# A fused attention and gated-FFN kernel on one core: the first block's keys summed by TensorE, its values by GpSimd, and a new order of all units

## The chip, the cores and the metric

One core of one Trainium2 chip. The metric is device time in microseconds, the median of several executions; a profile is one further execution, recorded by the hardware. PE is TensorE (matmuls; PEld its weight loads), DVE is VectorE, ACT is ScalarE, POOL is GpSimd, SP is SyncE, which here only issues DMAs.

## The reference

```python
# q, k, v: (8 batches, 8 heads, 576 tokens, 64); pool = 8, so 72 keys a head
k_p = k.reshape(B, H, 72, 8, D).mean(axis=3)
v_p = v.reshape(B, H, 72, 8, D).mean(axis=3)
scores = matmul(q, k_p.T) / sqrt(D);  attn = softmax(scores)
x = matmul(attn, v_p)  ->  (4608 tokens, 512)
out = (sigmoid(x @ w_gate) * (x @ w_val)) @ w_out      # 512 -> 1536 -> 512
```

## The kernel before

The 4608 tokens are worked in nine blocks of 512. Blocks 1 to 8 go in pairs, by seven products of half-size matrices in place of eight. The first block, `first_pass`, goes alone and plainly, since nothing else can run yet. Each large product takes three matmuls (high by high, high by low, low by high), because every operand is split in a high part, rounded to the matmul's faster type (fp32r), and a low part, the remainder. The weights come as 64-bit numbers and are converted on chip in four steps a piece (`step`, names `raw`, `w`, `parts`).

The first block, heads in four pairs p = 0 to 3, runs thus:

- `first` loads the pair's keys, its queries, the values and a matrix of zeros and ones (`in_sums`).
- `keys` (L1232) sums eight tokens each: one VectorE reduction of 128x576 to 128x72 a pair. The layout has channels on partitions.
- `place_keys` (L1236) scales the sums into the block-diagonal tile `kbd`, two ScalarE instructions a pair.
- `scores` multiplies queries by `kbd` (tiles `sc`, two halves a pair); `maximum`, `exps` and `total` make the softmax on VectorE and ScalarE; `main` and `rest_parts` scale the probabilities, those of the first 64 keys (`main`) and of the last eight (`rest`) apart.
- `sum_v` (L1334) sums the values on TensorE with the matrix of zeros and ones, tokens on partitions: eight fp32 matmuls into `vp` for the first 64 keys of all pairs, four into `vr` for the last eight. `v_hi` and `v_lo` copy them out.
- `turn_main` and `turn_rest` transpose the probabilities on TensorE (`tp`, `tr`), `product_av` multiplies them by the values (`av`), `x_of` copies the result as x's high part into `xo` on ScalarE, and `x_low` (L1420) subtracts it from `av` on VectorE for the low part.
- Then the products with the weights begin: matmuls named `chain`. The first of them, `whole("G", 1, 0)`, needs both parts of x of pairs 0 and 1 in its first half and of pairs 2 and 3 in its second.

An fp32 matmul takes two passes of the array, so that the trace shows two records for each; an fp32r matmul takes one.

The order of the work is written out. The words of `ORDER` say in which order the first block's steps are recorded, and all instructions of the kernel are recorded as units in a list. `LATER`, a table of 3800 numbers, then says in which order these units are issued. Each engine runs its own instructions strictly in that order, waiting where an operand isn't there. All recorded instructions pass through one helper and so have one line, L317; they are told apart by their tiles. Tile names: `early` and `h` are regions that serve as the first block's workspace (queries, maxima, probabilities, sums), `raw` and `raws` are landing places, `pm` and `e` probabilities. At the start TensorE runs seven fp32 matmuls without use (`idle`).

Of the kernel before, what the change touches and what calls it, by code (L numbers as in the profile page):

```python
# [11 lines left out]
F32 = mybir.dt.float32  # L12
# [7 lines left out]
P = 128  # L20
# [30 lines left out]
SIZE = {"k": S, "q": BT, "V": DM, "R": DM, "U": 360}  # L51

PLACE = {"k0": (0, 0), "k1": (0, 576), "k2": (0, 1152), "k3": (0, 1728),
         "q0": (0, 2304), "q1": (0, 2816), "q2": (0, 3328), "q3": (1, 0), "V0": (1, 512), "V1": (1, 1024), "V2": (1, 1536),
# [7 lines left out]
TURNED = {4: ((0, 2), (2, 4)), 5: ((0, 2), (2, 3), (3, 4)), 6: ((0, 3), (3, 4)), 7: ((0, 3), (3, 4)), 8: ((0, 4),)}  # L62
SMALL = {1: 0, 6: 6, 7: 7}

ORDER = """
first.0.3 first.1.0 first.0.1 first.0.0 first.0.2 first.1.2 first.3.1 first.3.3 first.1.1 keys.0.3 first.3.0 first.2.0
put.0.3 first.3.2 first.3.4 keys.0.1 lw.0.0@0 keys.0.0 put.0.1 lq.2.3@0 first.1.3 keys.0.2 put.0.0 lw.1.1@1 lw.0.1@2
sc.0.0.1@0 put.0.2 lv.1.1@1 sc.0.0.0@1 max.0.0.1 lw.1.0@3 sc.0.2.0@2 max.0.0.0 exp.0.0.1 lk.1.1@9 sc.0.2.1@3 max.0.2.0
lq.2.2@2 sc.0.1.1@4 max.0.2.1 lq.1.0@3 sc.0.1.0@5 lr.2.0@4 max.0.1.1 max.0.1.0 exp.0.2.0 lr.1.0@5 exp.0.1.0 pv@6,7
exp.0.1.1 lq.1.2@6 exp.0.0.0 lk.2.2@10 lv.1.2@7 exp.0.2.1 sum.0.0 lk.1.0@11 lv.2.3@8 conv.0.0@5 conv.0.0 rest.0.0  # L70
sc.0.3.1@0 conv.0.0 main.0.0 vhi.0.3 sc.0.3.0@2 max.0.3.1 again.0.0 vlo.0.3 exp.0.3.1 rturn.0.0@5 max.0.3.0 main.0.1
turn.0.0@4 conv.0.0 rcopy.0.0 hi.0.0 exp.0.3.0 lo.0.0 kw.0.0 turn.0.1@1 lw.1.3@4 sum.0.1 hi.0.1 conv.1.1@6 conv.0.0@7
rest.0.1 vhi.0.0 conv.0.0 main.0.3 conv.0.0@8 vlo.0.0 again.0.1 vhi.0.2 rturn.0.1@3 lo.0.1 vhi.0.1 av.0.0@0 main.0.2
rcopy.0.1 vlo.0.1 turn.0.3@5 conv.1.0@9 conv.0.0 av.0.1@4 vlo.0.2 x.0.0 keys.1.1 turn.0.2@2 x.0.1 xl.0 hi.0.3 lr.1.1@9
xl.1 hi.0.2 conv.1.0 lo.0.3 lo.0.2 av.0.3@1 conv.0.1@10 conv.1.0 av.0.2@3 conv.1.0 x.0.3 x.0.2 xl.3 kw.1.0 conv.1.0@11
xl.2 ol.0@0 conv.0.1 conv.0.1 mm.0.1@6 conv.1.1 conv.0.1 conv.1.1 conv.0.1@12 kw.0.1 lw.0.2@3 conv.0.1 conv.0.1@13
# [34 lines left out]

LATER = """
6 5 4 7 0 11 3 2 21 8 25 27 19 28 14 18 23 31 22 20 9 26 13 35 17 36 33 1 10 40 45 76 39 37 12 48 47 52 16 55 32 66 38
41 53 67 30 62 42 58 29 68 63 61 43 15 64 83 54 74 46 88 75 71 80 72 98 137 85 124 78 113 110 112 81 89 101 100 97 102
99 60 84 92 105 106 90 82 107 73 131 108 79 115 128 116 120 111 94 126 93 117 96 95 59 121 87 198 104 129 139 206 141
122 145 144 103 143 205 123 142 136 86 138 130 158 91 109 148 119 146 204 125 135 133 154 155 156 153 134 152 132 223
140 162 150 167 149 165 127 163 157 217 164 151 147 168 159 190 171 160 170 244 175 161 166 56 172 191 169 178 180 173
174 118 179 57 194 187 181 231 182 224 183 245 234 200 197 207 203 201 193 202 210 186 185 34 189 226 50 192 196 177
184 176 237 188 241 248 235 240 227 239 251 246 252 218 260 249 258 283 243 254 213 259 280 253 284 277 65 262 233 287
268 238 212 270 44 279 51 257 275 220 269 255 278 219 267 266 232 276 273 242 281 222 300 289 299 285 229 306 228 230  # L120
286 293 114 303 290 282 294 256 236 274 291 295 317 304 247 301 327 333 305 330 302 334 336 288 312 319 332 331 328
329 318 335 199 308 353 309 307 310 315 261 313 323 316 326 363 325 354 209 365 292 324 367 346 314 340 347 339 349
366 322 350 297 400 341 311 361 351 216 69 377 362 406 343 298 359 342 215 344 70 345 264 368 296 383 356 348 338 374
265 371 381 225 271 375 272 376 337 378 372 387 357 386 355 388 358 396 399 373 397 394 412 398 49 404 393 403 392 208
369 413 401 364 418 407 411 408 420 370 405 379 410 402 419 389 417 390 409 414 415 425 321 427 320 448 426 24 424 382
428 380 263 447 430 423 385 421 435 384 195 422 445 431 221 458 438 436 432 579 467 484 437 442 486 444 453 450 452
493 211 429 470 471 468 469 494 465 214 462 463 464 451 433 434 498 487 391 441 501 488 416 449 502 439 457 585 485
472 499 473 481 482 491 440 459 518 478 474 503 250 483 479 461 480 514 466 522 492 475 500 476 455 454 531 591 489
532 533 528 511 490 477 523 525 395 446 529 526 686 524 505 508 530 527 541 496 547 497 506 517 546 460 515 520 507
495 456 512 443 535 545 543 534 504 578 513 542 552 549 521 536 557 519 558 550 559 77 583 597 568 561 569 571 537 572  # L130
612 570 565 544 604 575 581 551 573 582 607 352 566 556 516 567 555 562 613 540 563 574 577 605 608 633 564 606 598
580 601 553 599 584 539 609 538 602 603 649 600 623 624 560 554 643 630 628 670 360 637 576 679 629 673 954 660 657
676 589 592 680 614 586 634 587 668 677 661 590 596 594 595 667 681 588 593 674 610 615 611 678 509 671 616 622 675
625 619 631 627 510 698 635 617 690 701 618 636 632 638 620 621 691 626 640 650 644 685 672 683 695 702 654 653 641
687 646 688 647 651 652 699 656 700 703 658 704 692 693 663 639 648 642 696 655 697 682 712 709 659 669 664 645 715
694 662 727 705 716 666 548 730 707 728 665 708 710 711 713 684 718 719 721 723 720 714 726 725 706 722 731 732 729
738 736 744 724 953 761 734 762 746 748 955 737 747 739 753 740 749 741 756 763 745 769 733 766 764 956 752 759 760
776 757 758 765 768 767 783 806 751 754 772 994 755 807 1102 773 788 778 771 775 784 770 790 785 796 777 801 789 798
717 780 802 781 808 786 794 742 793 774 800 805 820 826 797 823 795 817 957 832 787 779 803 816 824 782 841 829 825
818 834 830 804 851 852 827 811 868 831 853 821 828 854 810 872 855 865 838 856 822 848 849 809 743 857 819 842 858  # L140
879 850 880 882 750 883 864 884 859 735 922 689 903 876 863 904 837 885 926 812 905 814 815 792 881 918 813 886 862
839 833 877 873 860 995 845 958 889 836 1057 844 997 846 890 843 866 921 887 867 869 892 959 900 891 993 871 906 861
1103 901 870 878 894 874 835 893 875 902 1104 840 962 1105 960 923 961 907 895 963 916 1107 896 996 924 979 1106 909
973 933 1049 980 925 1047 982 847 919 897 888 1048 898 974 910 942 899 934 908 912 939 943 983 935 1111 981 927 936
930 913 984 914 1112 937 1108 1113 950 791 1050 998 1109 920 1114 940 1110 999 1167 1000 1051 944 1003 1052 911 1001
1002 970 1058 928 1135 938 917 1023 1064 941 915 945 1024 1094 951 947 964 946 965 1059 948 952 966 1168 1028 985 967
1025 968 1027 1026 988 1169 1031 969 1172 1032 949 989 931 1010 1170 1014 932 1171 976 1471 986 1136 1060 1176 1011
1063 1075 1173 1041 971 1175 977 987 1174 799 990 1012 978 1018 1013 1042 1177 991 1179 1029 1134 972 992 1183 1137
1178 1033 1255 1043 1030 929 1061 975 1004 1076 1015 1069 1019 1053 1044 1138 1020 1005 1045 1080 1035 1021 1046 1016
1007 1070 1022 1054 1008 1006 1139 1055 1184 1065 1034 1038 1009 1140 1071 1062 1081 1085 1039 1072 1186 1090 1040  # L150
1125 1073 1086 1257 1082 1056 1074 1145 1095 1256 1182 1143 1258 1117 1247 1144 1017 1142 1083 1087 1036 1260 1115
1084 1118 1037 1066 1151 1261 1116 1067 1141 1262 1119 1088 1153 1152 1147 1128 1146 1154 1239 1068 1237 1155 1156
1238 1157 1077 1263 1158 1129 1078 1185 1098 1099 1187 1079 1096 1180 1188 1126 1190 1100 1120 1191 1159 1189 1259
1101 1192 1130 1121 1181 1097 1089 1201 1264 1240 1091 1164 1202 1211 1241 1265 1203 1204 1148 1131 1267 1161 1291
1127 1198 1206 1318 1132 1205 1212 1133 1221 1162 1219 1242 1220 1160 1163 1226 1222 1231 1199 1092 1214 1248 1193
1093 1334 1333 1243 1122 1266 1232 1165 1251 1123 1249 1253 1215 1217 1207 1166 1252 1149 1216 1150 1227 1278 1320
1218 1319 1472 1234 1223 1270 1228 1224 1194 1233 1229 1124 1299 1323 1321 1301 1335 1213 1235 1324 1371 1336 1268
1236 1250 1322 1300 1208 1338 1292 1269 1244 1337 1370 1339 1195 1281 1200 1196 1209 1272 1287 1197 1245 1305 1230
1282 1225 1283 1331 1246 1342 1343 1273 1340 1341 1275 1254 1332 1274 1352 1327 1276 1353 1295 1315 1362 1328 1306
# [167 lines left out]


@with_exitstack
def attention_then_ffn(ctx: ExitStack, tc: tile.TileContext, qT, kT, vm, vr, vn, sums8, wgv, wo, const, out, outT):  # L330
    book = Book()
    nc = Core(tc.nc, book)

# [258 lines left out]
    def load(*what):  # L592
        return fill(rawp.tile([P, S], F32, name="raw"), *what)
# [984 lines left out]
```

## Time and profile before

| | us |
|---|---|
| median of three runs | 905.88 (904.68 to 906.97) |
| the profiled execution, its own time | 906.25 |
| its span, first to last instruction | 904.5 |
| PE busy in the span | 893.6 (99%) |
| DVE busy | 657.4 (73%) |
| ACT busy | 497.1 (55%) |
| POOL busy | 199.4 (22%) |

The profiled execution's own time is 1.8 us above its span, and 0.4 us above the median of the runs. A busy time counts records whose ends are modelled, since matmuls are pipelined; a pace is better read from starts.

### The profile page before, as it was taken

To read this page: it belongs to the slowest core of one execution; us is meant where nothing else is said; L and a number is where in the kernel's file an instruction comes from. 1 tells how busy PE (TensorE), PEld (TensorE's weight loads), DVE (VectorE), ACT (ScalarE), POOL (GpSimd) and SP (SyncE) were. 2 spreads that over 40 slices of the span, in tenths; PEclk is the share of its full clock that TensorE was granted. 3 is DMA by queue.
4 is the path that set the end of the run, shared out by engine and by line. 5 is a ranking of instruction groups with operands and counts; after the bars stand their busy time and mean duration, and the time that the engine had idled before them with its cause. 6 is when DMAs were issued, how large, how long until landed. Compare 5 with 4: busy or idle time off the path is not lost.

```text
span 904.5 us, 12612 instructions
## 1 busy us (share of the span) xinstructions
PE 893.6 (99%) x4162; PEld 735.1 (81%) x4162; DVE 657.4 (73%) x1039; ACT 497.1 (55%) x1071; POOL 199.4 (22%) x369
## 2 busy tenths in 40 slices
PE   7999999999999999999999999999999999999998
PEld 6788778888888888888888888888888888888886
DVE  7989788889899998757678796356589552224863
ACT  5888887587856475445365554334355542224352
POOL 2412101011164235443343104132213000000000
PEclk9999999999999999999999999999999999999999
DMA  9899888889999888787987787686747775746644
GB/s 342 302 332 349 289 331 303 299 280 330 329 328 313 278 288 287 234 304 260 302 273 245 243 279 260 225 269 198 256 127 249 247 251 201 227 169 205 195 167 141
DMA packets 100289, 237.56 MB, mean 263 GB/s; under 512 B 13856, under 2 KB 34720, under 8 KB 98688
## 3 DMA queue, kind: packets, MB, share of 16 engines
q1 hardware_dynamic: 85040, 203.84, 66.7%
q0 software_dynamic: 15040, 32.79, 10.6%
q8 instruction: 33, 0.54, 0.2%
q14 instruction: 32, 0.26, 0.1%
q10 hardware_dynamic: 144, 0.13, 0.0%
HBM read 176.02 MB, written 60.69 MB: 262 GB/s over the span
## 4 chain that ended last, share of the span: by engine, by line
PE 90%; DVE 4%; DMA 3%; ACT 2%; issue 1%; SPq 0%; DVEq 0%; ACTq 0%
PE chain L317 55%; PE acc L317 27%; PE av L317 4%; PE sc L317 3%; DVE early L317 1%; DMA raw<-in_wgv 1%; DMA raw_o<-in_wo 1%; PE tp L317 1%; DMA raw<-in_vr 1%; DMA h<-in_kT 0%; ACT e L317 0%; DVE s L317 0%; DVE hs L317 0%; DVE h L317 0%; ACT hs L317 0%
## 5 line engine op out<-in xcount | busy, mean ns | idle before, releaser
L317 PE MATMUL chain<-xo,parts 128*128 128x512 f32 x2316 | 543.7, 392 | 0.0
L317 PEld LDWEIGHTS chain<-xo,parts 128*128 128x128 f32 x2316 | 430.7, 188 | 92.5 <-issue 1.0
L317 PE MATMUL acc<-hs,oparts 128*128 128x512 f32 x1008 | 237.3, 391 | 0.3 <-issue 0.2
L317 PEld LDWEIGHTS acc<-hs,oparts 128*128 128x128 f32 x1008 | 188.0, 188 | 40.9 <-issue 1.2
L317 POOL DMA_DIRECT2D turned<-turn x240 | 131.7, 551 | 214.8 <-DVE turn L317 185.2
L317 DVE TENSOR_TENSOR y<-chain,sV 128x512 f32<-128x512 f32 x46 | 31.1, 686 | 69.3 <-PE chain L317 59.0
L317 DVE TENSOR_TENSOR hs<-h,hs 128x1024 fp32r<-128x1024 f32 x52 | 63.0, 1217 | 11.6 <-ACT hs L317 11.4
L317 ACT CAST hs<-h 128x1024 fp32r<-128x1024 f32 x52 | 54.4, 1050 | 30.0 <-PE acc L317 23.1
L317 ACT COPY chain<-chain 128x512 f32<-128x512 f32 x46 | 26.4, 576 | 57.0 <-PE chain L317 47.3
L317 DVE TENSOR_TENSOR y<-chain,sG 128x512 f32<-128x512 f32 x46 | 31.2, 682 | 34.0 <-PE chain L317 23.4
L317 ACT CAST hs<-s 128x1024 fp32r<-128x1024 f32 x36 | 37.5, 1051 | 28.4 <-PE acc L317 13.0
L317 ACT COPY sG<-chain 128x512 f32<-128x512 f32 x46 | 26.7, 586 | 46.5 <-PE chain L317 44.8
L317 DVE TENSOR_TENSOR hs<-s,hs 128x1024 fp32r<-128x1024 f32 x36 | 43.8, 1219 | 11.2 <-ACT hs L317 10.9
L317 ACT COPY sV<-chain 128x512 f32<-128x512 f32 x46 | 26.7, 585 | 38.8 <-PE chain L317 36.1
L317 DVE SCALAR_TENSOR_TENSOR h<-gate,chain 128x512 f32<-128x512 f32 x46 | 30.6, 677 | 21.8 <-PE chain L317 21.7
L317 ACT ACTIVATE gate<-chain 128x512 f32<-128x512 f32 x46 | 26.9, 594 | 34.2 <-PE chain L317 31.7
L317 PE MATMUL sc<-kbd,raw 128*128 128x144 f32 (+1 forms) x262 | 41.2, 296 | 0.1
L317 PEld LDWEIGHTS sc<-kbd,raw 128*128 128x128 f32 (+1 forms) x262 | 33.6, 176 | 7.9 <-issue 2.8
L317 ACT ACTIVATE gate<-y 128x512 f32<-128x512 f32 x46 | 28.9, 633 | 19.1 <-DVE y L317 19.0
L317 PE MATMUL acc<-oparts,hs 128*128 128x512 f32 x144 | 38.7, 402 | 0.2 <-ACT oparts L317 0.2
L317 DVE TENSOR_REDUCE m<-sc 128x4 f32<-128x288 f32 x48 | 21.7, 452 | 18.2 <-PE sc L317 17.7
L317 DVE SCALAR_TENSOR_TENSOR h<-gate,y 128x512 f32<-128x512 f32 x46 | 31.0, 683 | 0.3
(211 smaller groups left out, 1073.8 us busy)
## 6 DMA issues: line engine op xcount, KB each, us to landing
oparts<-keptS SPq DMA_DIRECT2D x48, 512.0 KB, 4.4
oparts<-keptO SPq DMA_DIRECT2D x72, 256.0 KB, 4.2
raw<-in_wgv SPq DMA_DIRECT2D x12, 1024.0 KB, 8.5
out<-o SPq DMA_DIRECT2D x35, 256.0 KB, 3.6
raw<-in_kT SPq DMA_DIRECT2D x28, 288.0 KB, 5.0
raw<-in_qT SPq DMA_DIRECT2D x29, 256.0 KB, 4.7
raw<-in_vm SPq DMA_DIRECT2D x24, 256.0 KB, 5.6
raw_o<-in_wo SPq DMA_DIRECT2D x12, 512.0 KB, 8.1
```

What stands on the lines that cost most here:

```text
L317: return self._book.take(lambda: f(*args, **named))
```

## The change

Four things change, all in the first block but the last.

- The keys of batch 0 come with tokens on partitions (`in_kn`), and a new `keys` sums them on TensorE: five fp32 matmuls a pair, four over 128 tokens with 16 columns of ones and one over 64 tokens with eight. All four pairs write one PSUM tile, `kp`. ScalarE's `place_keys` reads that tile.
- The values of batch 0 come with channels on partitions, as those of the other batches do. GpSimd sums the first 64 keys' values in three halving additions (`v_tree`), the last split over the two heads: four instructions a pair, 16 in all, and four memsets (`clear_v`) before. The eight matmuls into `vp` and the four ScalarE copies go. The `vr` matmuls stay, with a smaller matrix.
- The low part of x: TensorE adds minus the high part to the PSUM bank of `av` (`x_less`, one fp32r matmul with a negated identity that `minus` makes on ScalarE), and ScalarE copies what is left. The four VectorE subtractions go.
- `ORDER` gets the new words, and `LATER` is another table of 3819 numbers. Rotating buffers (`raw`, `y`, `m`) get written-out places.

```diff
@@ -60,10 +61,11 @@
+LESSENED = (0, 1, 2, 3)
...
@@ -109,162 +111,169 @@
 LATER = """
-6 5 4 7 0 11 3 2 21 8 25 27 19 28 14 18 23 31 22 20 9 26 13 35 17 36 33 1 10 40 45 76 39 37 12 48 47 52 16 55 32 66 38
...
@@ -1230,8 +1251,24 @@
         def keys(j, p):
-            k = raws["k", j, p] if j else got[f"k{p}"].rearrange("p (g t) -> p g t", t=POOL)
-            nc.vector.reduce_sum(out=ks[j, p][:, :KEYS], in_=k, axis=AX.X)
+            if j:
+                nc.vector.reduce_sum(out=ks[j, p][:, :KEYS], in_=raws["k", j, p], axis=AX.X)
+                return
+            if "k" not in vp:
+                vp["k"] = ps.tile([P, PAIRS, KEYS], F32, name="kp", tag=CHAIN[5])
...
+            with book.unit():
+                for c in range(4):
+                    nc.tensor.matmul(
+                        vp["k"][:, p, 16 * c:16 * c + 16], lhsT=got[f"k{p}"][:, c * P:(c + 1) * P], rhs=ones,
+                        start=True, stop=True,
+                    )
...
@@ -1333,28 +1370,30 @@
         def sum_v():
 
-            vp["m"] = bank_for([P, PAIRS, 2, D], "vp")
...
+        def v_tree(p):
+            v = got[f"V{p}"].rearrange("p (d t) -> p d t", t=POOL)
+            for n in (4, 2):
+                nc.gpsimd.tensor_tensor(out=v[:, :, :n], in0=v[:, :, :n], in1=v[:, :, n:2 * n], op=ALU.add)
+            for r in (slice(0, D), slice(D, P)):
+                nc.gpsimd.tensor_tensor(
+                    out=vh0[p][r, r].rearrange("p (d t) -> p d t", t=1), in0=v[r, :, :1], in1=v[r, :, 1:2], op=ALU.add
+                )
...
@@ -1417,8 +1454,20 @@
+        def minus():
+            nc.scalar.activation(phs[0][:, :P], ident, AF.Copy, scale=-1.0)
+
+        def x_less(p):
+            t = xo[(1, 2)[p // 2]]
+            nc.tensor.matmul(
+                av[0, p], lhsT=phs[0][:, :P], rhs=t[:, 0, p % 2], start=False, stop=True, skip_group_check=True
+            )
+
         def x_low(p):
             t = xo[(1, 2)[p // 2]]
+            if p in LESSENED:
+                nc.scalar.copy(t[:, 1, p % 2], av[0, p])
+                return
             nc.vector.tensor_tensor(out=t[:, 1, p % 2], in0=av[0, p], in1=t[:, 0, p % 2].bitcast(F32), op=ALU.subtract)
```

TensorE's first instructions in the kernel before, from its start (`kbd_89` to `kbd_92` are the placed keys of pairs 0 to 3; `h` holds keys and queries):

```order
L317 MATMUL idle<-kbd_93 128x144 x7
L317 MATMUL sc<-kbd_89,h 128x144 x4
L317 MATMUL sc<-kbd_90,h 128x144 x4
L317 MATMUL sc<-kbd_91,h 128x144 x4
L317 MATMUL vr<-xs_220 96x2x64 x4
```

And TensorE's first instructions in the changed kernel; the pairs of the `kp` matmuls are 3, 0, 1 and, after the scores of two pairs, 2:

```order
L326 MATMUL idle<-kbd_93 128x144 x7
L326 MATMUL kp<-h 128x16 x4
L326 MATMUL kp<-h 128x8
L326 MATMUL kp<-h 128x16 x4
L326 MATMUL kp<-h 128x8
L326 MATMUL kp<-h 128x16 x4
L326 MATMUL kp<-h 128x8
L326 MATMUL sc<-kbd_89,h 128x144 x4
L326 MATMUL sc<-kbd_90,h 128x144 x4
L326 MATMUL kp<-h 128x16 x4
L326 MATMUL kp<-h 128x8
L326 MATMUL sc<-kbd_91,h 128x144 x4
```

Three units of key sums now stand ahead of the first scores. The third of them carries a wait for ScalarE's third event, which is `place_keys` of pair 0: it writes the PSUM tile that ScalarE reads there.

TensorE at the end of the first block in the kernel before, from the product of pair 1 to the first `chain` (`vres_107` belongs to pair 3, `vres_106` to pair 2; `sc` with `raw` are scores of the next block):

```order
L317 MATMUL av<-pr,vres_105 128x512
L317 MATMUL tr<-identr,r_262 96x128 x2
L317 MATMUL tp<-cst,early 128x128 x3
...
L317 MATMUL sc<-kbd_93,raw 128x144
L317 MATMUL av<-early_219,early 128x512
L317 MATMUL av<-other,vres_107 128x512
L317 MATMUL sc<-kbd_93,raw 128x144 x2
L317 MATMUL av<-early_219,early 128x512
L317 MATMUL av<-other,vres_106 128x512
L317 MATMUL chain<-xo_269,parts 128x512 x6
```

The same place in the changed kernel; `av<-xo_269,ph` are the new subtractions for pairs 0 and 1:

```order
L326 MATMUL av<-xo_269,ph 128x512
L326 MATMUL tr<-identr,r_262 96x128 x4
L326 MATMUL tp<-cst,early 128x128 x4
L326 MATMUL sc<-kbd_93,raw 128x144 x2
L326 MATMUL sc<-kbd_89,raw 64x144
L326 MATMUL sc<-kbd_93,raw 64x144
L326 MATMUL sc<-kbd_93,raw 128x144
L326 MATMUL av<-early_219,early 128x512
L326 MATMUL av<-other,vres_107 128x512
L326 MATMUL av<-early_219,early 128x512
L326 MATMUL av<-other,vres_106 128x512
L326 MATMUL chain<-xo_269,parts 128x512 x6
```

What stands between the last transposes and the first `chain` is the same work in another order; the two subtractions of pairs 0 and 1 stand ahead of these transposes, and the two of pairs 2 and 3 behind the first six `chain` matmuls.

GpSimd in the changed kernel, the last of its value sums (in the kernel before none of the `early` and `xs` rows is there; `kbd_93` is a key tile of the next block, whose sums VectorE makes):

```order
L326 TENSOR_TENSOR early<-early 128x64x4
L326 TENSOR_TENSOR early<-xs_220 64x64
L326 TENSOR_TENSOR early<-early 128x64x2
L326 TENSOR_SCALAR w_250<-w_250 128x1024
L326 TENSOR_TENSOR early<-early 64x64
L326 TENSOR_SCALAR kbd_93<-early 64x72 x2
L326 TENSOR_TENSOR early<-early 64x64
L326 TENSOR_SCALAR w_267<-w_267 128x1024
```

The last addition, which completes the values of pair 2, now stands behind a weight conversion and behind the placing of the next block's keys.

## Rows read from the trace of the kernel before

**Rows 1.** The page, part 1: busy us, share of the span, instructions.

```profile
PE 893.6 (99%) x4162; PEld 735.1 (81%) x4162; DVE 657.4 (73%) x1039; ACT 497.1 (55%) x1071; POOL 199.4 (22%) x369
```

**Rows 2.** Stretches A:B: length, busy us of each engine, clock, DMA share, GB/s.

```profile
7.20:27.30 20.10, 17.09 (x97) 12.51 (x96) 19.72 (x47) 14.04 (x30) 4.93 (x6) 1.00 1.03 382
27.30:904.50 877.20, 870.97 (x4047) 717.32 (x4045) 635.47 (x990) 480.55 (x1035) 191.81 (x343) 1.00 0.77 260
```

**Rows 3.** Timeline of PE: start, us, instruction, xcount [idle before <-releaser].

```profile
1.67 3.73 PE L317 MATMUL idle<-kbd 128*128 128x144 f32 x14 [1.67 <-POOL kbd L318]
5.30 3.28 PE L317 MATMUL sc<-kbd,h 128*128 128x144 f32 x16
9.74 1.25 PE L317 MATMUL sc<-kbd,h 128*128 128x144 f32 x8 [1.16 <-ACT kbd L317]
...
23.20 0.51 PE L317 MATMUL tp<-cst,early 128*128 128x128 f32 x3
...
24.61 1.02 PE L317 MATMUL av<-early,early 128*128 128x512 f32 x2
...
25.70 0.65 PE L317 MATMUL sc<-kbd,raw 128*128 128x144 f32 x4
26.20 1.02 PE L317 MATMUL av<-early,early 128*128 128x512 f32 x2
...
27.29 1.09 PE L317 MATMUL chain<-xo,parts 128*128 128x512 f32 x4
```

**Rows 4.** The chain that ended last, its first long piece: start, us, what.

```profile
2.12 4.28 DMA h<-in_kT
```

**Rows 5.** Timeline of DVE, first 28 us.

```profile
3.75 1.48 DVE L317 TENSOR_REDUCE early<-h 128x72 f32<-128x576 f32 x2 [3.75 <-DMA h<-in_kT]
6.42 0.75 DVE L317 TENSOR_REDUCE early<-h 128x72 f32<-128x576 f32 x1 [1.19 <-DMA h<-in_kT]
7.09 0.45 DVE L317 TENSOR_REDUCE early<-sc 128x4 f32<-128x288 f32 x1
...
8.32 0.74 DVE L317 TENSOR_REDUCE early<-h 128x72 f32<-128x576 f32 x1
...
20.99 0.68 DVE L317 TENSOR_TENSOR early<-early 128x512 f32<-128x512 f32 x1
21.70 0.29 DVE L317 TENSOR_TENSOR vres<-vr,vres 32x128 fp32r<-32x128 f32 x1
22.02 0.37 DVE L317 TENSOR_TENSOR r<-rest,r 128x128 fp32r<-128x128 f32 x1
...
23.88 0.43 DVE L317 CAST parts<-w 128x512 fp32r<-128x512 f32 x1
24.34 0.69 DVE L317 TENSOR_TENSOR xo<-av,xo 128x512 fp32r<-128x512 f32 x1
...
25.38 0.64 DVE L317 CAST parts<-w 128x512 fp32r<-128x512 f32 x1
```

**Rows 6.** Timeline of ACT, the first placing of keys.

```profile
4.61 0.53 ACT L317 ACTIVATE kbd<-early 64x72 f32<-64x72 f32 x2 [2.36 <-DVE early L317]
```

**Rows 7.** Timeline of PE at 84.8 us, the shortest fp32 passes of the trace.

```profile
84.83 0.33 PE L317 MATMUL av<-early 128*128 128x64 f32 x2
84.97 0.28 PE L317 MATMUL av<-other,vres 96*128 96x64 f32 x1
```

**Rows 8.** Timeline of POOL, 24 to 36 us.

```profile
24.46 1.27 POOL L317 TENSOR_TENSOR parts<-w,parts 128x512 fp32r<-128x512 f32 x1 [2.06 <-DVE parts L317]
...
28.26 0.38 POOL L317 TENSOR_SCALAR kbd<-early 64x72 f32<-64x72 f32 x1
...
32.84 1.47 POOL L317 TENSOR_SCALAR kbd<-early 64x72 f32<-64x72 f32 x1
```

**Rows 9.** Waits of PE over the whole span: waited for, us, times, longest.

```profile
PE tp L317 <- ACT y L317: 0.7, 1, 0.7
...
PE av L317 <- DVE pl L317: 0.5, 1, 0.5
```

## What I expect of the change

> **What bounds the kernel now.** I read the page's first part, then the table of stretches, then the waits, and only then the start. The page puts PE at 99% of the span [rows 1], so a wait elsewhere counts only if PE waits with it. The table splits the span at the first `chain`. From 27.3 to 904.5 PE is busy 870.97 of 877.20 us, at a granted clock of 1.00 [rows 2]: 6.2 us are idle, and these hold the tail behind the last matmul and the waits. The two longest single waits there are 0.7 and 0.5 us [rows 9]. So whatever the new table of numbers does behind the first block, it can't win more than these few microseconds. The first 27.3 us are the soft part: between 7.2 and 27.3 PE is busy 17.09 of 20.10 us, DVE 19.72 [rows 2]. DVE is the bound there, and the reader should see in its timeline that from 6.42 us on it hardly stops [rows 5]. Since the same products follow in either kernel, the prediction is first of all the start of the first `chain`, 27.29 us [rows 3].
>
> What starts DVE is a transfer. The third key tile takes 4.28 us and lands at 6.40 [rows 4]; DVE waits 1.19 us for it, reduces it at 6.42, and takes its first maximum at 7.09 [rows 5], though the scores for that were begun at 5.30 [rows 3]. GpSimd is busy 4.93 of these 20.10 us [rows 2]: it has room.
>
> **The change part by part.** *Keys on TensorE.* DVE loses three reductions ahead of the first maximum, and a fourth behind it (8.32, 0.74 us [rows 5]). In their place PE has five fp32 matmuls a pair, ten passes. It starts them behind the 14 idle passes, which go from 1.67 to about 5.2, 0.26 each, while four fp32 records of the same shape at full clock take 0.5 from start to start (25.70 to 26.20), 0.125 a pass [rows 3]: the start runs at the lower of the two levels, 1.2 GHz, and the record from 7.2 on shows 2.4 [rows 2]. The first scores are those of pair 0, and its sums stand behind those of pair 3: 20 passes before ScalarE can place it. No row shows a pass of 16 columns with 128 columns of weights. The nearest is one of 64 columns at full clock: two take 0.14 (84.83 to 84.97), 0.07 each [rows 7]. Lower bound: 0.07 for all, 1.4 us, done at 6.6. Upper bound: each costs as much as one of 144 columns at the clock of its time, 0.25 until 7.2 and 0.125 after, done at 8.7. I take the nearest row at the clock of its time, 0.14 until 7.2 and 0.07 after: 14 passes and six, done at 7.6.
>
> The rule in the Trainium skill that speaks to this is in "TensorE: Matmul & The Clock Gate", section "LDWEIGHTS (loading the stationary operand)": a weight load's time goes by its columns and not by what is streamed past, P/1.2 ns. By it a short stream doesn't make a short pass: 128 columns make 107 ns, and 20 passes 2.1 us, an estimate from that page; my 2.4 lies beside it, and the sum would be 0.3 us lower.
>
> Then ScalarE places pair 0 (0.53 for two instructions [rows 6], with 0.1 for each hand-over: 8.3). The third unit of sums, of pair 1, writes the PSUM tile that ScalarE reads, and by the order it waits for that; it stands ahead of the first scores on PE. So ten passes at 0.07 come next, to 9.0, and then four passes of scores at 0.125 [rows 3]: the first maximum at about 9.5. Before it was 7.09. **Start of DVE's run: +2.4.**
>
> *DVE's run.* From its first maximum to the end of the last 128x512 product of `main` it takes 14.58 us before (7.09 to 20.99 + 0.68 [rows 5]). After, one reduction of 0.74 is gone from it, and two steps that stood behind (`vres` 0.29, `r` 0.37 [rows 5]) stand within: 14.5. It ends at 24.0, in place of 21.67, if it is never kept waiting. But before, PE came to the last transposes only at 23.20 [rows 3], 1.5 us after DVE had finished; in the changed kernel PE will wait here, and start at 24.1. **Last transposes: +0.9.** From there to the first `chain` stood 4.1 us of work (23.20 to 27.29 [rows 3]); the same matmuls but for a few scores stand between them now, 3.9: first `chain` at 28.0. **+0.7.**
>
> *Values on GpSimd.* Eight matmuls into `vp` (16 passes) leave PE in a stretch in which it has 3 us to spare [rows 2]: worth nothing. On GpSimd an addition of 512 columns takes 1.27 where its operands are split in two types, and a scaling of 64x72 takes 0.38, or 1.47 in a worse moment [rows 8]. The tree has, for each pair, 256 columns, 128 and two of 64 rows by 64: by the share of columns about 0.65, 0.4 and 2x0.38, 1.8 a pair, 7.3 for four. The values land around 12 us, as the old ones did, so 19.5 to 21.6 with the weight conversion that stands between. The last addition, of pair 2, waits longer: it is queued behind the placing of the next block's keys, whose reduction DVE makes just ahead of its last product, at about 23.3. That gives 25.3 with three small instructions, and the product of pair 2 comes at 28.0 - 1.1 = 26.9. **Hidden, with 1.6 us to spare**; without that cover it costs what it is late.
>
> What GpSimd may cost is DVE's pace: one cast to `parts` takes 0.43 on DVE at 23.88 and 0.64 at 25.38, the second while GpSimd has its 1.27 addition [rows 5, 8]. If all 7.3 us of the tree slowed DVE like this, a third, that were 2.4; the tree's small pieces stand apart and DVE's reads of PSUM make half of its run, so the bounds are 0 and 1.5; I take **+0.4**.
>
> *Low part of x.* DVE loses four subtractions of 0.69 [rows 5], all behind its critical run; PE gets four fp32r matmuls of 512 columns, 0.27 each (four `chain` matmuls of that form: 1.09 [rows 3]). Two stand ahead of the last transposes, where PE waits anyhow; two behind the first `chain` matmuls. **+0.5**, between 0 (if a wait covers them) and 1.1.
>
> *The new table.* Some of the 1.2 us of the two named waits [rows 9] may go and as much may come: the order has no durations, so nothing there says which. Bounds -1.2 and +1.0; **-0.3**.
>
> Sum: 0.7 + 0.4 + 0.5 - 0.3 = +1.3, on the profiled execution's 906.25: 907.55. That execution is 0.37 above the median of the runs, so I state **907.2**.
>
> **The rivals.** *A, faster.* The start isn't late: the sums cost the lower bound (1.0 us less), GpSimd leaves DVE alone (0.4 less), and the 1.2 us of waits go. The chain of DVE's run can give back at most 0.7, since ahead of 23.2 PE was the later one; so 907.2 - 0.7 - 0.4 - 0.9 = 905.2, and 903.5 if subtractions and further small waits lie hidden too. For it: DVE has 2.7 us less work. Against: that work lies behind its run, or in the wait for the third key tile.
>
> *B, slower, by the clock.* Before, PE had scores of 144 columns from 5.30, then full clock at 7.2 [rows 2, 3]. After, it has in that time passes of 16 columns with little streamed, and a wait of 0.7 for ScalarE. If full clock comes only behind the first scores, the ten passes of pair 1 and the first scores run at 0.14 and 0.25: 0.7 + 0.5 later, and the six passes of pair 0 0.4 later, 1.6 in all: 908.8, or 909.6 if DVE's run waits for the next scores by as much as half of that again. It decides if the level is still 1.2 GHz at 11 us. [...]
>
> *C, slower, by GpSimd.* The tree takes twice my estimate, 14.6 us, as the 1.47 beside the 0.38 [rows 8] suggests. Then the last values come at some 28.9 and the product of pair 2 is 2 us late: 909.2. It decides at 8.9 us for the tree and its waits.
>
> **How the numbers follow.** Within 0.3% is 903.2 to 908.6, about what a measurement can tell here. Chances: my sum 0.5, A 0.25, B 0.15, C 0.10. A lies below 903.2 for half of its weight, 0.13 faster; B and C lie above 908.6 for most of theirs, with little of the sum's upper edge 0.21 slower; 0.66 within. The range takes in A's end and B's: 903.0 to 910.2; the sum's own is 905.5 to 908.9, by its terms' bounds taken together by halves.
>
> **What the profile would show.** Right: the first maximum at 9.5 (9.0 to 10.6), PE waiting for DVE ahead of the last transposes, the first `chain` at 28.0, the tree's 16 additions in about 7.3 us of busy time, DVE's long products at 0.68 beside it. Wrong: a first `chain` at 27.0 or earlier; PE waiting for GpSimd at a product of values; granted clock at half in the stretch from 7.2 to 11; or a difference in the table of waits behind the first block of more than 1.2 us, which my sum holds for impossible.

## The result and the profile after

The changed kernel took 914.33 us (median of 4, 911.83 to 917.89) against 905.28 for the kernel before on the same chip: a ratio of 1.0093, interval 1.0075 to 1.0111. It is slower, and by 9 us where 1.3 were forecast. The profiled execution took 911.83, its span 909.8; the other executions' spans go up to 916.1.

The page's first part, whose counterpart is [rows 1]:

```profile
PE 897.7 (99%) x4190; PEld 740.0 (81%) x4190; DVE 655.5 (72%) x1031; ACT 499.3 (55%) x1072; POOL 208.4 (23%) x389
```

TensorE has 4.1 us more work by it, GpSimd 9.0. Most of the loss shows in the start. The timeline of TensorE (columns as in [rows 3]):

```profile
1.67 3.52 PE L326 MATMUL idle<-kbd 128*128 128x144 f32 x14 [1.67 <-POOL kbd L327]
5.59 2.69 PE L326 MATMUL kp<-h 128*128 128x16 f32 x20 [0.41 <-DMA h<-in_kn]
8.90 2.42 PE L326 MATMUL kp<-h 128*128 128x16 f32 x10 [0.61 <-ACT kbd L326]
11.24 4.09 PE L326 MATMUL sc<-kbd,h 128*128 128x144 f32 x16
15.17 1.28 PE L326 MATMUL kp<-h 128*128 128x16 f32 x10
...
29.11 0.66 PE L326 MATMUL tp<-cst,early 128*128 128x128 f32 x4
...
32.63 0.47 PE L326 MATMUL av<-other,vres 96*128 96x512 f32 x1 [0.34 <-DVE vres L326]
...
34.03 1.56 PE L326 MATMUL chain<-xo,parts 128*128 128x512 f32 x6
```

Ten passes of the key sums cost 1.28 us in one place and 2.42 in another, though they are the same instructions. The table of stretches (columns as in [rows 2]) says why:

```profile
7.00:8.00 1.00, 1.00 (x9) 0.97 (x9) 0.00 (x0) 0.00 (x0) 0.00 (x0) 1.00 1.07 414
8.00:9.00 1.00, 0.39 (x3) 0.29 (x3) 0.00 (x0) 0.45 (x2) 0.00 (x0) 0.63 1.06 387
9.00:10.00 1.00, 1.00 (x6) 1.00 (x6) 0.00 (x0) 0.00 (x0) 0.00 (x0) 0.50 1.06 242
...
14.00:15.00 1.00, 1.00 (x6) 1.00 (x5) 1.00 (x4) 0.21 (x1) 0.65 (x3) 0.50 1.01 383
15.00:16.00 1.00, 1.00 (x10) 1.00 (x9) 0.75 (x3) 0.47 (x1) 0.33 (x1) 0.96 1.05 395
```

The granted clock was 1.00 (2.4 GHz) while the first twenty passes ran, fell to 0.50 (1.2 GHz) behind them, and came back at about 15 us, behind the scores of two pairs. In the kernel before it was 1.00 from 7.2 on [rows 2], and eight passes of scores took 1.25 us there [rows 3]. VectorE's timeline:

```profile
12.61 0.46 DVE L326 TENSOR_REDUCE early<-sc 128x4 f32<-128x288 f32 x1 [12.61 <-PE sc L326]
13.56 0.46 DVE L326 TENSOR_REDUCE early<-sc 128x4 f32<-128x288 f32 x1 [0.50 <-PE sc L326]
...
18.71 0.57 DVE L326 TENSOR_SCALAR early<-early 128x16 f32<-128x16 f32 x1
...
28.37 0.69 DVE L326 TENSOR_TENSOR early<-early 128x512 f32<-128x512 f32 x1
...
30.75 1.41 DVE L326 CAST parts<-w 128x512 fp32r<-128x512 f32 x1
32.19 0.29 DVE L326 TENSOR_TENSOR vres<-vr,vres 32x128 fp32r<-32x128 f32 x1
```

The sum from these lines and [rows 3, 5] (`early<-sc` is the first maximum, the product at 28.37 the last long one of the run): the first maximum is 5.52 us later (12.61 for 7.09). VectorE's run from there to the end of the last long product takes 16.45 in place of 14.58, +1.87. From that end to the first `chain` it is 4.97 (29.06 to 34.03) in place of 5.62 (21.67 to 27.29), -0.65. Together +6.74, which is the first `chain` at 34.03 for 27.29. Behind it stand 875.8 us to the end of the span, before 877.2; in all fifteen profiles of this case that stretch takes 875.5 to 878.3, wherever the first `chain` stands, so their spans differ mostly by the start.

### The profile page after: what moved, and what is told of

Same layout as the page of the kernel before. It is cut to its first block, busy times and chain, and to the rows that moved or that the text cites. A ratio compares the mean times of both kernels' runs of the same rounds, so it can differ in the third digit from the quotient of the medians.

```text
span 909.8 us, 12667 instructions
## 1 busy us (share of the span) xinstructions
PE 897.7 (99%) x4190; PEld 740.0 (81%) x4190; DVE 655.5 (72%) x1031; ACT 499.3 (55%) x1072; POOL 208.4 (23%) x389
## 4 chain that ended last, share of the span: by engine, by line
PE 92%; ACT 2%; DVE 2%; DMA 2%; issue 1%; POOL 0%; SPq 0%; DVEq 0%; POOLq 0%; ACTq 0%
PE chain L326 54%; PE acc L326 29%; PE sc L326 4%; PE av L326 4%; DMA raw<-in_qT 1%; PE kp L326 1%; PE tp L326 1%; DMA keptG0D<-parts 1%; DMA h<-in_kn 0%; DVE early L326 0%; DVE h L326 0%; ACT early L326 0%; DVE parts L326 0%; ACT e L326 0%; ACT w L326 0%
```

## The experiments

Each was timed against the kernel before on the same chip; its median in these runs was 905.65 to 906.57.

**The changed kernel again** (no edit), timed, and once more for a profile.

> The changed kernel once more, unaltered. In its first profile the granted clock is 0.50 from about 8.3 to 15.0 us, and the first chain stands at 34.03 in place of 27.29. Theory 1 (the clock: the key sums' passes let TensorE fall back to its lower level ahead of the first scores): the same fall is in this profile too, perhaps at another time, and the first maximum stands at 11 to 14 us. Rival (the fall was an accident of that one execution): the clock stays at 1.00 from about 7 us on, the first maximum stands at 10.5 to 11, and the time is near that of before plus 4.

> The changed kernel once more, for a third profile: its unprofiled times were up to 4 us above those of the two profiles. If the clock's first rise and its fall move from execution to execution, this profile shows another stretch at 0.50 and a span that follows it.

916.12 us, ratio 1.0107 (1.0087 to 1.0126). In both profiles the clock falls as in the first: 0.54 and 0.56 in 8 to 9 us, 0.50 to 14; the first `chain` stands at 33.64 and 33.45, +6.4 and +6.2. Of that the first maximum (11.85 and 11.87) makes +4.8, not +5.5: the first profile's key sums began 0.65 later, with a wait of 0.41 for keys that the two others don't have. VectorE's run takes 16.81 and 16.60. The fall is no accident. But it did not move in the third profile as that expectation held possible: what the executions with spans to 916.1 do differently is not seen in these three.

**Keys back on VectorE**, all else changed.

```diff
-            if "k" not in vp:
-                vp["k"] = ps.tile([P, PAIRS, KEYS], F32, name="kp", tag=CHAIN[5])
...
+            k = raws["k", j, p] if j else got[f"k{p}"].rearrange("p (g t) -> p g t", t=POOL)
+            nc.vector.reduce_sum(out=ks[j, p][:, :KEYS], in_=k, axis=AX.X)
...
-                    nc.scalar.activation(t[r, c], vp["k"][r, p], AF.Copy, scale=SCALE)
+                    nc.scalar.activation(t[r, c], ks[j, p][r, :KEYS], AF.Copy, scale=SCALE)
```

> The changed kernel with the keys summed by VectorE as before, all else as changed. Theory 1 and every theory that puts the loss on the key sums: first maximum at about 7.1 us, first chain at 26.5 to 27.5, and with the 875.8 us that stand behind the first chain in the changed kernel a time 0.5 to 3 us below before. Rival (the loss lies in the values on GpSimd, the low part or the new order): 908 or more.

909.89, ratio 1.0041 (1.0028 to 1.0054): 6.2 us below the changed kernel beside it, but not at or below the kernel before. The key sums are the larger part, not all. In TensorE's timeline one wait stands out:

```profile
6.77 2.20 PE L326 MATMUL sc<-kbd,h 128*128 128x144 f32 x16 [1.38 <-DMA h<-in_qT]
11.58 1.29 PE L326 MATMUL sc<-kbd,h 128*128 128x144 f32 x8 [2.61 <-ACT kbd L326]
```

The new order has no early place for the fourth reduction on VectorE. The clock then fell behind this wait, 0.50 from 13 to 19 us. First `chain` at 29.59.

**Wide passes**: the same key matmuls stream 128 columns, 16 of ones and 112 of zeros.

```diff
-            ones = got["k3"][:, 640:656]
+            ones = got["k3"][:, 640:768]
...
-                        vp["k"][:, p, 16 * c:16 * c + 16], lhsT=got[f"k{p}"][:, c * P:(c + 1) * P], rhs=ones,
+                        vp["k"][:, b + 16 * c:b + 16 * c + 128], lhsT=got[f"k{p}"][:, c * P:(c + 1) * P], rhs=ones,
```

> The changed kernel with the same key passes, each of which streams 128 columns (16 of ones, 112 of zeros) in place of 16. Theory 1 (the narrow streams let the clock fall): granted clock 1.00 throughout, a pass still near 0.13 us, first maximum at about 10.8 in place of 12.6, first chain near 31, 2 to 4 us faster than the changed kernel. Rival 2 (the loss is the 30 passes' price by their weights, the clock adds little): the same time as the changed kernel, within 1 us. Rival 3 (the clock falls for the waits between the units): it falls here as well.

912.13, ratio 1.0079 (1.0058 to 1.0099); the changed kernel beside it 1.0107, so the intervals overlap a little and the time alone is weak. TensorE's timeline isn't:

```profile
5.19 3.20 PE L327 MATMUL kp<-h 128*128 128x128 f32 x20
9.00 1.57 PE L327 MATMUL kp<-h 128*128 128x128 f32 x10 [0.62 <-ACT kbd L327]
10.50 2.23 PE L327 MATMUL sc<-kbd,h 128*128 128x144 f32 x16
...
31.86 1.57 PE L327 MATMUL chain<-xo,parts 128*128 128x512 f32 x6
```

```profile
11.29 0.95 DVE L327 TENSOR_REDUCE early<-sc 128x4 f32<-128x288 f32 x2 [11.29 <-PE sc L327]
```

The wait of 0.62 for ScalarE is still there, and yet the scores run at 2.4 GHz: sixteen passes in 2.23 us in place of 4.09. The first maximum came at 11.29, the first `chain` 1.6 to 2.2 us earlier than in the three profiles of the changed kernel. So the wait by itself doesn't bring the clock down (rival 3), and the passes' place and price stay when the clock is held: the first maximum is still 4.2 us late, in passes that are a little dearer (0.15 to 0.16 for 0.13). VectorE's run takes 15.59 here.

**A bank of their own for pairs 1 and 2.**

```diff
-                vp["k"] = ps.tile([P, PAIRS, KEYS], F32, name="kp", tag=CHAIN[5])
+                vp[side] = ps.tile([P, PAIRS, KEYS], F32, name="kp", tag=CHAIN[5 if p in (3, 0) else 4])
```

> The changed kernel with the sums of pairs 1 and 2 in a PSUM bank of their own, so that the third unit doesn't wait 0.6 us for ScalarE's placing of pair 0. Rival 3 (the wait breaks TensorE's work and brings the clock down): clock 1.00 and 3 us or more faster than the changed kernel. Theory 1: the clock falls all the same; 0 to 0.7 us faster.

913.84, ratio 1.0084 (1.0068 to 1.0100), overlapping with the changed kernel's 1.0087 to 1.0126; the first `chain` at 32.23. Without any wait between the thirty passes the clock fell all the same: 0.88 in 8 to 9 us, 0.50 from 9 to 12. It fell once more later, 0.60 in 22 to 24 us.

```profile
5.19 4.18 PE L326 MATMUL kp<-h 128*128 128x16 f32 x30
9.29 3.62 PE L326 MATMUL sc<-kbd,h 128*128 128x144 f32 x16
```

**One part alone on the kernel before.** Four kernels, each with one of the four changes.

> The kernel before with the keys of the first block summed by TensorE, nothing else changed and the order of before kept. Theory 1 (the key sums are the main cost, by their passes and by the clock that falls behind them): first maximum at 10.5 to 13 us in place of 7.09, 4 to 9 us slower than before. Rival (the keys cost what was forecast, about +1, and the loss comes only with the new order): 0 to 2 us slower.

Keys (the code of the diff ahead of the prediction, the order of before): 918.51, ratio 1.0136 (1.0123 to 1.0149). This is more than the part can be charged with: the matrix of ones comes in pair 3's tile, which the old order loads last, and TensorE waits for it. The clock was 0.50 from 9 to 25 us.

```profile
8.13 2.38 PE L318 MATMUL kp<-h 128*128 128x16 f32 x10 [3.04 <-DMA h<-in_kn]
```

> The kernel before with the values of the first block summed by GpSimd, nothing else changed; the 16 additions stand in GpSimd's order where the changed kernel has them. Theory 2 (GpSimd's additions slow the VectorE instructions beside them and hold back GpSimd's placing of the next keys): first chain 0.5 to 2 us later than 27.29, time 0.5 to 2 us over before. Rival (the additions are hidden): within 0.5 us of before.

Values on GpSimd (`v_tree`, `clear_v`; the eight `vp` matmuls go): 909.61, ratio 1.0044 (1.0027 to 1.0060). The first `chain` came at 30.48, in a profiled execution that was the fastest of the seven (907.77). Here TensorE was idle where the value sums had stood, and its clock fell:

```profile
21.16 1.09 PE L318 MATMUL tp<-cst,early 128*128 128x128 f32 x4 [2.73 <-DVE early L318]
```

```profile
18.00:20.00 2.00, 0.43 (x4) 0.29 (x4) 1.87 (x5) 2.00 (x5) 1.76 (x4) 0.84 1.03 350
20.00:25.00 5.00, 3.85 (x8) 2.25 (x9) 4.93 (x8) 2.55 (x6) 4.70 (x8) 0.50 0.99 400
```

> The kernel before with the low part of x made by TensorE and ScalarE, nothing else changed; each subtraction and copy stands where the VectorE subtraction stood. Four more matmuls of 0.27 on a TensorE that is nearly always busy: 0 to 1.2 us over before. Rival (VectorE's four freed 0.69 us let the next scores start earlier): up to 1 us under before.

Low part (`minus`, `x_less`, copies on ScalarE): 908.42, ratio 1.0028 (1.0018 to 1.0039). First `chain` at 28.73, and TensorE then waits for ScalarE's copies (columns as in [rows 9]):

```profile
PE chain L319 <- ACT xo L319: 0.8, 2, 0.5
```

Not all of the 1.44 us at the first `chain` are the low part's: 0.37 are a key transfer that landed later (first maximum 7.46), 0.29 VectorE's run (14.87), and only 0.78 lie behind it, where its new matmuls begin. TensorE ran at the lower level to about 10 us in this start, 24 passes of scores in 5.34 us, though nothing of the low part stands there and the table of stretches says 1.00:

```profile
6.12 5.34 PE L319 MATMUL sc<-kbd,h 128*128 128x144 f32 x24 [0.72 <-DMA h<-in_qT]
```

> The new order of all units with the keys on VectorE, the values on TensorE and the low part on VectorE, as before. With the keys alone undone the new order was 3.8 us over before, its scores of the third pair waiting 2.6 us for a late key reduction and the clock falling behind that wait. Theory 3 (the new order, drawn up for other work, costs this, whatever does the values): 2 to 4 us over before, with the same wait. Rival (the values on GpSimd and the low part make these 3.8): within 1 us of before.

The new order with none of the three: 919.04, ratio 1.0150 (1.0131 to 1.0170). This tells nothing of the order that the changed kernel has: I had to find places for the four copies of the value sums, which the new order lacks, and put them on ScalarE ahead of the exponentials. There VectorE waits 5.04 us:

```profile
26.09 0.75 DVE L330 TENSOR_REDUCE early<-early 128x8 f32<-128x576 f32 x1 [5.04 <-ACT early L330]
```

I count this one as failed. Whether the new order costs or wins in itself was not settled.

**Sums later**: only those of pair 0 ahead of the first scores, with narrow and with wide passes. In `LATER` the sums of pair 1 move behind the scores of pair 0, those of pairs 3 and 2 behind the scores of pair 1; pair 3 gets a bank of its own.

```diff
...
+            bank = "k3" if p == 3 else "k"
+            if bank not in vp:
+                vp[bank] = ps.tile([P, PAIRS, KEYS], F32, name="kp", tag=CHAIN[4 if p == 3 else 5])
```

> The changed kernel with only the sums of pair 0 ahead of the first scores; those of pair 1 stand behind these, those of pairs 3 and 2 behind the scores of pair 1 (pair 3 in a bank of its own). 20 passes and the wait for ScalarE go from ahead of the first maximum. Theory 1 (the place and the price of these passes, in the start that DVE waits for): first maximum at 8 to 9.5 in place of 12.6 or 11.5, first chain 2.5 to 4 us earlier, 2 to 4 us faster than the changed kernel (910 to 913). Rival (the loss lies behind the start: GpSimd beside VectorE and a clock that falls later): less than 1 us of it comes back.

> The same with passes of 128 columns in place of 16. Theory 1 with the clock: 1.00 from its first rise on, first chain as in the run beside it or up to 2 us earlier. Rival (the clock does not matter once the scores stand between the sums): the same time, within 1 us.

Narrow: 918.09, ratio 1.0129 (1.0111 to 1.0147). Wide: 912.73, ratio 1.0070 (1.0054 to 1.0087). The intervals are apart: 5.4 us for the columns alone. TensorE, narrow:

```profile
5.19 2.25 PE L331 MATMUL kp<-h 128*128 128x16 f32 x10
8.05 2.29 PE L331 MATMUL sc<-kbd,h 128*128 128x144 f32 x8 [0.62 <-ACT kbd L331]
10.13 2.25 PE L331 MATMUL kp<-h 128*128 128x16 f32 x10
...
22.43 2.02 PE L331 MATMUL vr<-xs 64*96 64x128 f32 x8
```

and wide:

```profile
5.16 1.46 PE L332 MATMUL kp<-h 128*128 128x128 f32 x10
7.24 1.25 PE L332 MATMUL sc<-kbd,h 128*128 128x144 f32 x8 [0.62 <-ACT kbd L332]
8.33 1.46 PE L332 MATMUL kp<-h 128*128 128x128 f32 x10
```

Eight passes of scores take 2.29 us in the first and 1.25 in the second: 1.2 and 2.4 GHz. With narrow passes TensorE never left the lower level until about 27 us, and I had expected this kernel to be faster than the changed one. Theory 1 in the form "place and price" was wrong in what it forecast here (the first maximum at 9.42 came 2 to 3 us earlier, the time went up), and right in the form "clock". The wide one had its first maximum at 8.04, yet its first `chain` only at 32.62, for VectorE then waits for scores behind the sums that stand between, and after that 1.24 and 0.68 for ScalarE: an earlier first maximum alone gives little.

```profile
11.20 0.95 DVE L332 TENSOR_REDUCE early<-sc 128x4 f32<-128x288 f32 x2 [1.48 <-PE sc L332]
```

Nor did the clock hold here "from its first rise on": it was 0.55 in 22 to 24 us and 0.60 in 24 to 26. That fall cost little: from the end of VectorE's run (27.51) to the first `chain` it is 5.11 us, 4.98 in the run with wide passes, where the clock held.

**Values on GpSimd, with work in TensorE's gap**: eight matmuls of the same size, unused, where the value sums stood.

```diff
+                            vp["m"][:, :, hd], lhsT=ident,
+                            rhs=got[f"q{c}"].rearrange("p (n h d) -> p n h d", h=2, d=D)[:, :, hd],
```

> The values alone on GpSimd, as run before (4.0 us over the kernel before, granted clock 0.50 from 19.7 to 26 us), with eight matmuls put back on TensorE where the value sums stood: the same size, on queries and the identity, their result unused. Theory 4 (the value sums that went had kept TensorE busy; without them the clock falls): clock 1.00 in 18 to 27 us, 2 to 3.5 us faster than without them. Rival (GpSimd's additions beside VectorE are the cost): within 1 us of the run without them.

908.85, ratio 1.0037 (1.0020 to 1.0053), not to be told from 1.0044 without them. The clock was 1.00 from 7 us on, the first `chain` at 29.98 in place of 30.48. So the fall of the clock there was real, but worth at most half a microsecond at the first `chain`, of which 0.17 stood already at the transposes ahead of it (20.99 for 21.16); the rival holds. The 2.7 us that remain at the first `chain` have their lines on GpSimd and VectorE:

```profile
26.56 0.90 PE L318 MATMUL sc<-kbd,raw 128*64 128x144 f32 x4 [1.10 <-POOL kbd L318]
```

```profile
22.71 1.33 DVE L318 TENSOR_TENSOR r<-rest,r 128x128 fp32r<-128x128 f32 x1
```

The next block's keys are placed behind the additions, so that its scores wait; and the `r` subtraction, 0.37 before [rows 5], takes 1.33 beside GpSimd's work. That work is not an addition but a weight scaling (22.86, 1.03 us), which stood at 16.04 in the kernel before and now comes behind the additions.

**Keys on VectorE with the old start**: as the second experiment, but transfers, reductions and placings in the order of before.

> The changed kernel with the keys on VectorE as before, and this time the first transfers, the key reductions and the placings in the order of before (the fourth reduction behind two maxima). In the earlier run without this the third pair's scores waited 2.6 us and the clock fell behind the wait. Theory 5 (beyond the key sums, the values on GpSimd and the low part on TensorE cost of themselves, 2 to 4 us): 908 to 910, with the first scores of the third pair near 10 us and no wait of 2.6. Rival (the late fourth reduction was the rest of the loss): within 1 us of before, 905.5 to 907.5.

908.86, ratio 1.0023 (1.0013 to 1.0034): without the late reduction 2.3 of the 3.8 us remain, with the keys out of play. Not all of that is the values' and the low part's own: the first scores wait 1.45 us for queries here, and the clock is low behind that. First `chain` at 29.93.

```profile
6.64 1.22 PE L331 MATMUL sc<-kbd,h 128*128 128x144 f32 x8 [1.45 <-DMA h<-in_qT]
```

```profile
12.00:16.00 4.00, 4.00 (x17) 3.45 (x17) 4.00 (x12) 1.53 (x6) 2.59 (x5) 0.50 1.00 384
```

No kernel tried beats the one before.

## Why the prediction was wrong

**The step that failed first** is "the nearest row at the clock of its time", 0.14 until 7.2 and 0.07 after, and on it "the first maximum at about 9.5". I took a pass of 64 columns as the measure of one of 16. Measured at 2.4 GHz: 20 passes from 5.59 to 8.28 and ten in 1.28, 0.13 each; at 1.2 GHz ten in 2.42, 0.24. That is what a pass of 144 columns takes (0.125 [rows 3] and 0.26): the columns streamed were not the price. The weight loads (PEld) fill nearly all of the time, nine of them 0.97 us of the stretch from 7 to 8, which makes them the likely price; no run had other weights. The 0.07 of [rows 7] was read from a place where they don't show: there the two loads begin while the long matmuls ahead still run.

```profile
84.38 0.62 PE L317 MATMUL acc<-oparts,hs 128*128 128x512 f32 x2
84.61 0.41 PEld L317 LDWEIGHTS av<-early 128*128 128x128 f32 x2
```

For the first twenty the lower level that I assumed hid the error (2.4 for 2.69, and a start 0.4 late for a transfer); for the third unit it stood bare, "ten passes at 0.07". The Trainium skill's rule ("TensorE: Matmul & The Clock Gate", "LDWEIGHTS (loading the stationary operand)") goes by the columns of the weights, 107 ns for 128. The trace agrees in kind, with about a fifth more at 2.4 GHz (0.13), and not at 1.2 GHz, where a pass took 0.24. I had named it and weighed it for the twenty alone; for the ten of the third unit it makes 1.1 in place of my 0.7, an estimate from that page. The upper bound, "as much as one of 144 columns", held for the twenty, done at 8.3 for 8.7.

**The clock** is rival B, with a chance of 0.15. It decided as written, "if the level is still 1.2 GHz at 11 us": it was 0.50 there in all three profiles of the changed kernel. Its course was another. I let the rise come late; in the profiles it came in time, fell behind the first twenty passes and stayed down through the third unit (2.42 us, for 1.28 at 2.4 GHz) and the first scores (1.37 us from their start to the first maximum, for 0.79 in the run with wide passes). The differences are 1.1 and 0.6, together 1.7 us of the first term. B has 1.6 for it, which is near by luck: 0.4 of that stood for six passes of pair 0 that ran at 2.4 GHz. First maximum 12.61, +5.5 (+4.8 in the two other profiles), where my sum and B together made +4.0. The rest of the term is the passes and their wait: the wide passes, with the clock held, still leave +4.2. The Trainium skill says ("TensorE: Matmul & The Clock Gate", Part 1) that throttled is the clock's default and that activity releases it. The two "sums later" runs agree with that in part: in the wide one TensorE came to 2.4 GHz ahead of the first scores, in the narrow one it stayed at 1.2 GHz to about 27 us, though no wait there was longer than 0.62 us.

**VectorE's run** was put at 14.5 and took 16.45. It waits for scores at the lower clock (0.50 at 13.56), which the run with wide passes doesn't; that one took 15.59. Part of the rest is single operations that stretch beside GpSimd's additions (0.57 for the 128x16 scaling, 0.17 in the run with wide passes). My +0.4 stood for this; the 1.1 that is left with the clock held lies under its upper bound of 1.5. The term "last transposes +0.9" followed these: 29.11.

**From there to the first `chain`** I counted 3.9 and it took 4.92: the product of pair 3 waits for `vres`, which stands behind the cast of 1.41 us, 0.43 and 0.64 before [rows 5]. A weight scaling on GpSimd (30.85, 1.03 us) runs beside it. The order showed the place, not the length.

**Hidden value sums.** "Worth nothing" for the matmuls taken from TensorE missed that a gap on TensorE went with a lower clock; alone, that was half a microsecond at most. The additions themselves came out near the forecast 7.3 us, 7.9 by GpSimd's rows, and the last ended in time:

```profile
29.86 1.01 POOL L326 TENSOR_TENSOR early<-early 64x64 f32<-64x64 f32 x1
```

The product of pair 2 came at 32.93, so rival C fell. What costs is beside them: the values alone 4.0 us (2.4 to 5.4). The low part, forecast at +0.5, cost 2.8 alone (1.6 to 3.5), in an order not drawn up for it; its profile shows less (0.8 ahead of the first `chain`, two waits of 0.8 together behind).

**The new table**: behind the first `chain` 875.8, and 878.2 and 877.7 in the two other profiles of the same kernel, before 877.2. A gain of 0.3 can't be seen in that. Rival A fell with the start.

**What stays open**: the medians lie 2.5 us above the changed kernel's profiled times. Spans of 914 to 916 with a recorded mean clock of 1.00 look like the narrow "sums later" run, whose span is 916.1 and which ran at the lower level to 27 us. But one span of 911.9 has 1.00 too, and one of 916.0 has 0.989, and none of these executions' traces was seen: this is a guess. The parts alone add up to more than the whole loss, since each was put into an order made for something else; their shares in the changed kernel are known only as 6.2 us for the keys and 2.3 to 3.8 for the rest.

## What to carry to other kernels

Price a small matmul by its weights until a row of its own shape, among others of its kind, shows otherwise; a short stream made no short pass here. Where TensorE's work changes its kind or gets a gap, ask whether the granted clock holds, and follow it to the work behind, which pays for it. Work moved to an engine with room costs its neighbours: look at what shares its time on VectorE, and at what is queued behind it.

## What the runs showed that I had not expected

The recorded clock can't be trusted ahead of its first change. In the narrow "sums later" run the table says 1.00 from the start:

```profile
16.00:18.00 2.00, 2.00 (x10) 1.94 (x10) 0.51 (x2) 0.57 (x3) 1.00 (x2) 1.00 1.09 440
```

but the passes there run at half the pace of the wide run (2.29 us for 1.25). So do the idle passes at the start of every profile, 0.25 each, and the first scores of the run with the low part alone, both under a recorded 1.00. The length of a known pass tells the level where the record has not begun.
